# Linear attention and a softplus MLP on one core: the first unit loaded in two transfers, fewer filler matmuls at the start, and another order of the last block's last two tiles

## The chip, the cores and the metric

One Trainium2 chip, one core. The metric is device time in microseconds (us) of one launch. The kernel before took 1006.22 us, the median of 3 runs (1006.0 to 1007.1).

## The reference

The inputs are q, k and v (8 batches, 8 heads, 576 tokens, 64 columns), omega (128 features x 64), and the two weight matrices of an MLP (512 x 2048 and 2048 x 512). Cut to what matters:

```python
def phi(x):                                  # x is q or k, scaled by 64 ** -0.25
    h = x @ omega.T - sum(x * x) / 2
    return exp(h - max(h)) / sqrt(128)
kv = einsum("bhsm,bhsd->bhmd", phi(k), v)
z = phi(k).sum(axis=2)
x = einsum("bhsm,bhmd->bhsd", phi(q), kv) / (einsum("bhsm,bhm->bhs", phi(q), z) + 1e-6)
h = x.reshape(4608, 512) @ w_in              # heads side by side
out = softplus(h) @ w_out                    # 4608 x 512
```

## The kernel before, in words

The host lays the inputs out so that each transfer is one rectangle of 128 partitions. The attention of a batch is worked in two **quads** of four heads, and a quad in five **units** of 128 tokens. For a unit of keys of the first batch one transfer (line 463, 128 x 772 words) brings three things side by side: 256 columns of the transposed inputs, which PE multiplies by omega (`project`, line 491, tile `ppk`); 256 columns of the same inputs by rows, which ACT squares (line 474) and DVE sums into norms (line 481); and v with a column of ones, which the outer product with the features uses (line 700, tile `kt`). From `ppk` DVE takes the maxima (line 541), forms two biases (lines 548 and 553, tile `smk`), and ACT takes the exponents (line 561) from PSUM into the unit's own tile. Each unit needs two PSUM banks for `ppk`, and there are eight banks, so the fifth unit's `project` waits for the exponents of the first one.

The MLP takes the tokens in blocks: two of 256, then blocks of 512. Layer 1 gives `h`, ACT and DVE make the softplus, split in a high and a low part (`gh`, `gl`, or both in `g`), and layer 2 (lines 1109 to 1111: high x high, high x low, low x high) adds into four accumulators `acc`, one per **tile** of 128 tokens, over 16 **steps** of 128 hidden columns. The last two blocks are worked together (`plan_both`). The very last one has all its `g` before layer 2 starts, so its layer 2 is written out as a list, `order`: tile after tile (tt = 0 to 3), 16 steps each. Only the last tile is different: steps 0 to 12 (`LATE` = 12) at full width into its accumulator, then steps 13 to 15 for the left 256 columns, then steps 13 to 15 for the right 256 columns into a bank of its own, `right`.

`plan_out` ends a tile: DVE copies the left half of the accumulator into an output tile `o` (line 1121), ACT the right half (line 1126), and SP stores it with two transfers of 64 rows (line 1139). For tile 3 of the last block ACT copies the right half of steps 0 to 12 early, DVE copies the left half when its steps end, and DVE adds the bank `right` at the very end (line 1130); each half then goes out in two transfers, one from SP and one from ACT's queue.

Nothing of the order is left to run time. All pieces of work are planned as `Work` with a cost, a due time, the engines that can do it and the buffers that it takes and gives back. `in_order` simulates the engines with these costs and writes the one order in which instructions are emitted. An output tile of the last block takes a buffer of the room "end" at its first copy and gives it back when its last store is planned to have landed. That room has four names; three of them (`ph.0` to `ph.2`) are held to the end of the program by the sums of `plan_both`, so one, `x.0`, is left.

`with_fill` then puts **filler matmuls** (line 1582, 128 x 128 of ones with no use, two instructions each) into PE's stream where the plan has PE idle: for a gap it counts the gap less `FILL`, divided by 0.2135 us, and ahead of each work that takes a bank before `DENSE` = 12 us of planned time it puts two more. Ten fillers stand ahead of everything else.

Of the kernel before, what the change touches and what calls it, by code (L numbers as in the profile page):

```python
# [24 lines left out]
DM = 512  # L25
DFF = 2048
NFC = DFF // P
# [8 lines left out]
MARGIN = 0.0000  # L36
START = {"SP": 0.75, "ACT": 1.9, "PE": 4.6}
SLOW = 7.19
FILL = 0.3
DENSE = 12  # L40
PATIENCE = {"PE": 0.0000, "DVE": 0.00, "ACT": 0.1822, "POOL": 0.00, "SP": 3.0950}
LEAN = {"DVE": 0.2675, "POOL": 0.1608, "ACT": 0.00}
SPREAD = ((0, 10.51), (17, 12.01))
VW = 512 + 4 * (D + 1)
# [8 lines left out]
LATE = 12  # L53
# [8 lines left out]
def by(key, due):  # L62

    return due + DUE[key][PHASE[0]]
# [192 lines left out]
def with_fill(out, held, banks, until, emit):  # L257

    last, all_ = None, []
    for i, w in enumerate(out):  # L260
        if w.engine == "PE":
            t = w.end - w.cost
            n = int((t - last - FILL) / 0.2135) if last is not None and t < until else 0
            if last is not None and t < DENSE and w.take:
                n += 2
            names = [
                b for b in banks if all(x1 <= last and g < i or x0 >= t and f >= i for x0, x1, f, g in held.get(b, []))
            ] if n > 0 else []
            names = names or [box[key] for _, box, key in w.take if box[key] in banks]
            if names and n > 0:  # L270
                all_.append((emit, names[0], n))
            last = w.end
        all_.append(w)
    return all_
# [3 lines left out]
def favor_softplus_kernel(ctx, tc, q0, k0, qx, kx, tx, vv, om, wi, wo, out):  # L278
    nc = tc.nc
# [10 lines left out]
    at = ctx.enter_context(tc.tile_pool(name="at", bufs=1))  # L290
# [4 lines left out]
    def bank(name, tag):  # L295
        return ps.tile([P, 512], F32, name=name, tag=tag, bufs=1)

    idle = at.tile([P, P], F32, name="idle", tag="x.0", bufs=1)
# [38 lines left out]
    def act(n, space=None):  # L337
        return (0.066 if space == PSUM else 0.105) + 0.000833 * n

    def dve(n, rate=1):  # L340
        return 0.068 + 0.001042 * n / rate
# [4 lines left out]
    def do(engine, cost, due, emit, **kw):  # L346

        on = dict(zip(engine, cost)) if isinstance(engine, tuple) else {engine: cost}
        w = Work(on, due, emit, **kw)
        works.append(w)  # L350
        return w
# [86 lines left out]
    def plan_unit(q, kind, us, due, early, other=None):  # L438

        u = us[0]  # L440
# [3 lines left out]
        if early:  # L444
            src = (k0 if kind == "k" else q0)[q.qd]
        else:
            src = (kx if kind == "k" else qx)[q.b - 1, q.qd]
        nt = 2 * len(us) if u < 4 else 2 if other else 1
        b2 = {}
        w, n = nt * P, 2 * nt  # L450
        b = {}

        def load():
            if early:

                x = const.tile([P, 2 * DM], F32, name=f"x{nm}", tag=b["x"], bufs=1)
                b["v"] = x[:, UW : UW + 4 * (D + 1)].rearrange("p (c d) -> p c d", d=D + 1)
                b["qt"] = x[:, UW : UW + 4 * P].rearrange("p (c t) -> p c t", t=P)
                b["xs"] = x[:, : 4 * D]
                b["ph"] = x[:, : n * M].rearrange("p (c m) -> p c m", m=M)  # L460
                b["raw"], b["nat"] = x[:, :w], x[:, w : 2 * w].rearrange("p (c d) -> p c d", d=D)
                if kind == "k":
                    nc.sync.dma_start(x[:, :VW], src[:, u * VW : (u + 1) * VW])
                else:
                    nc.sync.dma_start(x[:, : 2 * w], src[:, u * UW : u * UW + 2 * w])
                return
            x = at.tile([P, 2 * UW], F32, name=f"x{nm}", tag=b["x"], bufs=1)
            nc.sync.dma_start(x[:, : 2 * w], tx[other.n - NQ] if other else src[:, u * UW : u * UW + 2 * w])
            b["raw"], b["nat"] = x[:, :w], x[:, w : 2 * w].rearrange("p (c d) -> p c d", d=D)
# [52 lines left out]
        def first(e, t):  # L522
            if not t:
                for i, x in enumerate(to):
                    x["ph"] = at.tile([P, k, M], F32, name=f"ph{nm}_{i}", tag=x["phs"], bufs=1)
            (nc.scalar.copy if e == "ACT" else nc.vector.tensor_copy)(features(t), b["pr", t][:, :, 0])
# [28 lines left out]
        def exponent(j):  # L555
# [7 lines left out]
        size = P * 4 * (VW if early and kind == "k" else 2 * w)  # L563
        ld = do(
            "SP", dma(size), by("unit.load", due), load, behind=prev.get("load"),
            take=[("w" if early else "x", b, "x")], delay=DL, spare=2 if early else 0,
        )
# [27 lines left out]
        else:  # L595
# [12 lines left out]
            for t in range(nt):  # L608
# [4 lines left out]
                c = do(  # L613
                    ("ACT", "DVE"), (act(2 * M, PSUM), dve(2 * M)), by("unit.first", due), lambda e, t=t: first(e, t), after=[p], behind=e,
                    take=[] if t else phs,
                )
# [536 lines left out]
    def plan_both(i, due, pace, box):  # L1153

        PHASE[0] = 2
        t7, t8, n = (B - 1) * MAIN, B * MAIN, TB
# [301 lines left out]
            plan_out(i, t7, tt, due + pace * NFC, acc[t7], box, [last7[tt]])  # L1458
        due += pace * NFC
        halves = [slice(k * DM // 2, (k + 1) * DM // 2) for k in range(2)]  # L1460
        order = [(tt, fc, slice(0, DM)) for tt in range(4) for fc in range(NFC if tt < 3 else LATE + 1)]
        order += [(3, fc, c) for c in halves for fc in range(LATE + 1, NFC)]
        ends = {tt: [] for tt in range(4)}
        for m, (tt, fc, c) in enumerate(order):
            w = c.stop - c.start
# [74 lines left out]
    for i, n in enumerate(sizes):  # L1540
        acc = []

        def starts(x):
            y = quads[x[1]]
            return y.b * MAIN + P * min(next(z for z in y.parts if u in z)[0] for u in x[3])

        while j < len(side) and any("q" in x[2] and starts(x) < t0 + n for x in side[j:]):
            due, m, kind, us, early = side[j]
            if kind == "kq":
                plan_unit(quads[m + 1], "k", us, due, early, quads[m])  # L1550
            else:
                plan_unit(quads[m], kind, us, due, early)
            j += 1
        boxes.append({} if i < 2 else dict(boxes[-1]))
        if t0 == (B - 1) * MAIN:
            plan_rest(at_due - 10.0)
            plan_both(i, at_due, JOINT, boxes[-1])
            break
        pace = 4.0 if i < 2 else PACE
        for fc in range(NFC):  # L1560
            plan_step(i, t0, n, fc, (FIRST + LATER * i if i < 2 else at_due) + pace * fc, pace, acc, boxes[-1])
        if i:
            at_due += (NEXT if i == 1 else pace * NFC)
        t0 += n
# [14 lines left out]
    def fill(tag, n, idle=ident):  # L1579
        t = bank("fill", tag)[:, :P]  # L1580
        for _ in range(n):
            nc.tensor.matmul(t, idle, idle, start=True, stop=True)  # L1582

    with tc.manual_schedule():
        fill("at.0", 10, idle)
        for w in with_fill(*in_order(works, room, AHEAD, MARGIN), room["any"], 70, fill):
            if isinstance(w, tuple):
                w[0](*w[1:])
                continue
            w.emit(w.engine) if len(w.on) > 1 else w.emit()  # L1590
# [99 lines left out]
```

## Time and profile before

| what | value |
|---|---|
| median of 3 runs | 1006.22 us |
| the profiled execution's own time | 1006.46 us |
| its span in the trace | 1004.7 us |
| busy PE, DVE, ACT | 992.0, 805.4, 673.7 us |
| chain that ended last: PE, DVE, ACT | 87%, 6%, 4% |

The profiled execution took 1.76 us more than its span, and 0.24 us more than the median. The chain that ended last is followed back from the last instruction, at each step to what released it, so its shares say on which engine the time was spent, and its rows say when. In the timeline a bracket gives how long the engine had been idle before the row and who ended that. Rows that follow each other on one line are merged, "x8" tells of how many. PE's matmuls overlap: their pace is read from start to start, not from their length. In these rows "PEclk" reads 1.00 throughout; a filler matmul nevertheless starts every 0.23 us in the first microseconds and every 0.13 us later, so the lower one of the clock's two levels (1.2 GHz) is read from the pace.

### The profile page before, as it was taken

What the parts mean: (1) busy time and instruction counts of PE and PEld (TensorE: products, weight loads), DVE (VectorE), ACT (ScalarE), POOL (GpSimd) and SP (SyncE); (2) the same over time, 40 slices, a digit from 0 to 9 for tenths busy, and PEclk for the clock granted to TensorE, in tenths of its full rate; (3) what the DMA queues carried; (4) which work ended last, traced back from release to release, by engine and by line L of the source; (5) the groups of instructions that cost most, each with busy time, mean ns of one, the idle gap of its engine ahead of it and who ended that gap; (6) DMA issues with size and microseconds to landing.
All of it is one profiled execution on the core that took longest, in us unless ns stands there. A gap on an engine that the chain in (4) does not pass through costs nothing.

```text
span 1004.7 us, 17142 instructions
## 1 busy us (share of the span) xinstructions
PE 992.0 (99%) x5753; PEld 807.7 (80%) x5753; DVE 805.4 (80%) x2194; ACT 673.7 (67%) x1629; POOL 79.8 (8%) x90
## 2 busy tenths in 40 slices
PE   9999999999999999999999999999999999999998
PEld 8888888787778787887878787878788778788886
DVE  6999997988868787888888897979889846998600
ACT  6999987757677675666675756756576555777600
POOL 0113211000001000100000000100010000001000
PEclk9999999999999999999999999999999999999999
DMA  9963444443252424442343335243534121000011
GB/s 346 373 242 118 146 151 122 134 117 94 96 149 95 134 93 132 137 114 82 115 120 126 91 95 152 95 132 94 133 117 112 64 79 42 1 1 1 1 53 32
DMA packets 64334, 113.81 MB, mean 113 GB/s; under 512 B 18268, under 2 KB 37112, under 8 KB 64248
## 3 DMA queue, kind: packets, MB, share of 16 engines
q1 hardware_dynamic: 64088, 112.60, 36.1%
q8 instruction: 46, 0.75, 0.3%
q14 instruction: 40, 0.33, 0.1%
q10 hardware_dynamic: 160, 0.13, 0.1%
HBM read 85.68 MB, written 27.03 MB: 112 GB/s over the span
## 4 chain that ended last, share of the span: by engine, by line
PE 87%; DVE 6%; ACT 4%; DMA 1%; issue 1%; POOL 0%; DVEq 0%; ACTq 0%; SPq 0%
PE acc L1109 13%; PE acc L1110 12%; PE acc L1111 12%; PE h L1049 10%; PE h L1050 9%; PE h L1051 9%; PE ppk L491 3%; PE kt L655 3%; PE xp L977 3%; PE pb L1384 2%; PE ppq L516 2%; PE pc L1384 2%; PE pa L1384 1%; DMA xq<-qx 1%; PE fill L1582 1%
## 5 line engine op out<-in xcount | busy, mean ns | idle before, releaser
L1109 PE MATMUL acc<-wo,gh 128*128 128x512 f32 x512 | 204.1, 399 | 0.0
L1110 PE MATMUL acc<-wo,gh 128*128 128x512 f32 x512 | 200.2, 391 | 0.0
L1111 PE MATMUL acc<-wo,gl 128*128 128x512 f32 x512 | 199.7, 390 | 0.0
L1049 PE MATMUL h<-xh,wi 128*128 128x512 f32 (+1 forms) x512 | 190.8, 373 | 1.9 <-DVE u L1064 1.1
L1050 PE MATMUL h<-xl,wi 128*128 128x512 f32 (+1 forms) x512 | 186.1, 364 | 0.0
L1051 PE MATMUL h<-xh,wi 128*128 128x512 f32 (+1 forms) x512 | 185.8, 363 | 0.0
L1055 ACT ACTIVATE u<-h 128x512 f32<-128x512 f32 (+1 forms) x128 | 70.1, 547 | 81.4 <-PE h L1051 79.2
L1109 PEld LDWEIGHTS acc<-wo,gh 128*128 128x128 f32 x512 | 96.2, 188 | 24.9 <-issue 6.8
L1049 PEld LDWEIGHTS h<-xh,wi 128*128 128x128 f32 x512 | 96.4, 188 | 23.4 <-DVE u L1064 3.9
L1111 PEld LDWEIGHTS acc<-wo,gl 128*128 128x128 f32 x512 | 96.1, 188 | 21.2 <-DVE gl L1204 0.4
L1110 PEld LDWEIGHTS acc<-wo,gh 128*128 128x128 f32 x512 | 96.5, 188 | 15.9
L1051 PEld LDWEIGHTS h<-xh,wi 128*128 128x128 f32 x512 | 96.4, 188 | 15.4
L1050 PEld LDWEIGHTS h<-xl,wi 128*128 128x128 f32 x512 | 96.6, 189 | 13.5
L1064 DVE SCALAR_TENSOR_TENSOR u<-h,u 128x512 f32<-128x512 f32 (+1 forms) x128 | 79.2, 619 | 32.7 <-ACT u L1061 31.5
L1068 ACT CAST gh<-u 128x512 fp32r<-128x512 f32 (+1 forms) x101 | 57.2, 566 | 46.0 <-PE acc L1110 29.1
L1072 DVE TENSOR_TENSOR gl<-u,gh 128x512 fp32r<-128x512 f32 (+1 forms) x106 | 68.7, 648 | 14.9 <-ACT gh L1068 13.1
L1061 ACT ACTIVATE u<-u 128x512 f32<-128x512 f32 (+1 forms) x128 | 74.2, 580 | 3.9
L1058 ACT ACTIVATE u<-u 128x512 f32<-128x512 f32 (+1 forms) x128 | 74.3, 581 | 3.2
L887 DVE CUSTOM_DVE_ANT_0 junk<-phq,zb 128x128 bf16<-128x128 f32 (+1 forms) x228 | 67.4, 296 | 7.0 <-ACT phq L561 0.4
L538 ACT ACTIVATE phq<-phq,smq 128x128 f32<-128x128 f32 x194 | 59.5, 389 | 10.1 <-DVE smq L553 10.1
L561 ACT ACTIVATE phk<-ppk,smk 128x128 f32<-128x128 f32 x230 | 63.6, 375 | 3.3 <-DVE smk L553 3.1
L541 DVE TENSOR_REDUCE smk<-ppk 128x4 f32<-128x512 f32 (+2 forms) x80 | 46.0, 595 | 24.5 <-PE ppk L491 24.5
(217 smaller groups left out, 1764.2 us busy)
## 6 DMA issues: line engine op xcount, KB each, us to landing
xk<-kx SPq DMA_DIRECT2D x28, 512.0 KB, 3.8
xq<-qx SPq DMA_DIRECT2D x28, 512.0 KB, 3.6
fdq<-flq SPq DMA_DIRECT2D x28, 512.0 KB, 2.8
qq<-fdq SPq DMA_DIRECT2D x112, 128.0 KB, 2.9
rawi<-wi SPq DMA_DIRECT2D x16, 512.0 KB, 6.7
rawo<-wo SPq DMA_DIRECT2D x16, 512.0 KB, 10.1
out<-o SPq DMA_DIRECT2D x32, 256.0 KB, 2.1
v<-vv SPq DMA_DIRECT2D x14, 576.0 KB, 3.7
```

The lines of the kernel that those rows point to most:

```text
L887: nc.vector.tensor_tensor_reduce(jk[r, c % jk.shape[1]], ph[r, c], q.zb[r, h], 1.0, 1e-6, ALU.mult, ALU.add, dn[r, 0, c : c + 1])
L1049: nc.tensor.matmul(b["h"], wh, xh[:, cc, t], start=cc == 0, stop=False)
L1050: nc.tensor.matmul(b["h"], wh, xl[:, cc, t], start=False, stop=False)
L1051: nc.tensor.matmul(b["h"], wl, xh[:, cc, t], start=False, stop=cc == NCC - 1)
L1055: nc.scalar.activation(b["u"], b["h"], AF.Abs)
L1058: nc.scalar.activation(b["u"], b["u"], AF.Exp, scale=-1.0)
L1061: nc.scalar.activation(b["u"], b["u"], AF.Ln, bias=1.0)
L1064: nc.vector.scalar_tensor_tensor(b["u"], b["h"], 0.0, b["u"], ALU.max, ALU.add)
L1072: (nc.vector if e == "DVE" else nc.gpsimd).tensor_tensor(b["gl"], b["u"], b["gh"].bitcast(F32), ALU.subtract)
L1109: nc.tensor.matmul(dst, gh, w2[fc][:, 0, c], start=start, stop=False, **kw)
L1110: nc.tensor.matmul(dst, gh, w2[fc][:, 1, c], start=False, stop=False, **kw)
L1111: nc.tensor.matmul(dst, gl, w2[fc][:, 0, c], start=False, stop=stop, **kw)
```

## The change

Three things are done. The transfer of the very first unit (quad 0, unit 0, keys) is cut in two, the 256 columns for PE first, then the other 516. Fillers: 6 instead of 10 ahead of everything, `FILL` is 1.0 instead of 0.3, and the two extra ones for works that take a bank are gone. And `order` of the last block: tile 2 stops after step 12, tile 3 goes up to step 12, then come steps 13 to 15 of tile 2, then those of tile 3's halves.

```diff
--- before.py
+++ after.py
@@ -36,8 +36,7 @@
 MARGIN = 0.0000
 START = {"SP": 0.75, "ACT": 1.9, "PE": 4.6}
 SLOW = 7.19
-FILL = 0.3
-DENSE = 12
+FILL = 1.0
 PATIENCE = {"PE": 0.0000, "DVE": 0.00, "ACT": 0.1822, "POOL": 0.00, "SP": 3.0950}
 LEAN = {"DVE": 0.2675, "POOL": 0.1608, "ACT": 0.00}
 SPREAD = ((0, 10.51), (17, 12.01))
@@ -261,8 +260,6 @@
         if w.engine == "PE":
             t = w.end - w.cost
             n = int((t - last - FILL) / 0.2135) if last is not None and t < until else 0
-            if last is not None and t < DENSE and w.take:
-                n += 2
             names = [
                 b for b in banks if all(x1 <= last and g < i or x0 >= t and f >= i for x0, x1, f, g in held.get(b, []))
             ] if n > 0 else []
@@ -460,7 +457,8 @@
                 b["ph"] = x[:, : n * M].rearrange("p (c m) -> p c m", m=M)
                 b["raw"], b["nat"] = x[:, :w], x[:, w : 2 * w].rearrange("p (c d) -> p c d", d=D)
                 if kind == "k":
-                    nc.sync.dma_start(x[:, :VW], src[:, u * VW : (u + 1) * VW])
+                    for c in ((0, w), (w, VW)) if not q.qd and not u else ((0, VW),):
+                        nc.sync.dma_start(x[:, c[0] : c[1]], src[:, u * VW + c[0] : u * VW + c[1]])
                 else:
                     nc.sync.dma_start(x[:, : 2 * w], src[:, u * UW : u * UW + 2 * w])
                 return
@@ -1458,7 +1456,8 @@
             plan_out(i, t7, tt, due + pace * NFC, acc[t7], box, [last7[tt]])
         due += pace * NFC
         halves = [slice(k * DM // 2, (k + 1) * DM // 2) for k in range(2)]
-        order = [(tt, fc, slice(0, DM)) for tt in range(4) for fc in range(NFC if tt < 3 else LATE + 1)]
+        order = [(tt, fc) for tt in range(2) for fc in range(NFC)] + [(tt, fc) for tt in (2, 3) for fc in range(LATE + 1)]
+        order = [(tt, fc, slice(0, DM)) for tt, fc in order + [(2, fc) for fc in range(LATE + 1, NFC)]]
         order += [(3, fc, c) for c in halves for fc in range(LATE + 1, NFC)]
         ends = {tt: [] for tt in range(4)}
         for m, (tt, fc, c) in enumerate(order):
@@ -1582,7 +1581,7 @@
             nc.tensor.matmul(t, idle, idle, start=True, stop=True)
 
     with tc.manual_schedule():
-        fill("at.0", 10, idle)
+        fill("at.0", 6, idle)
         for w in with_fill(*in_order(works, room, AHEAD, MARGIN), room["any"], 70, fill):
             if isinstance(w, tuple):
                 w[0](*w[1:])
```

The fillers on PE fall from 10, 1, 1, 1, 6, 5, 2, 18, 1 to 6, 0, 0, 0, 1, 0, 0, 15, 0; the one of 18 stands some 61 us into the program. Nothing else of any engine's order changes between the start and the last block. The rows below are from PE around the fifth and sixth unit (`ppk_0_2`: quad 0, unit 2), first before, then with the change.

```order
L491 MATMUL ppk_1_1_1_160<-omf,xk_1_1_112 128x128
L1582 MATMUL fill<-ident 128x128 x6
L491 MATMUL ppk_0_2_0_189<-omf,xk_0_2_123 128x128
L491 MATMUL ppk_0_2_1_190<-omf,xk_0_2_123 128x128
L491 MATMUL ppk_0_2_0_189<-omf,xk_0_2_123 128x128
L491 MATMUL ppk_0_2_1_190<-omf,xk_0_2_123 128x128
L1582 MATMUL fill<-ident 128x128 x5
L491 MATMUL ppk_1_2_0_216<-omf,xk_1_2_137 128x128
L491 MATMUL ppk_1_2_1_217<-omf,xk_1_2_137 128x128
L491 MATMUL ppk_1_2_0_216<-omf,xk_1_2_137 128x128
L491 MATMUL ppk_1_2_1_217<-omf,xk_1_2_137 128x128
```

```order
L489 MATMUL ppk_1_1_1_151<-omf,xk_1_1_109 128x128
L1581 MATMUL fill<-ident 128x128
L489 MATMUL ppk_0_2_0_175<-omf,xk_0_2_120 128x128
L489 MATMUL ppk_0_2_1_176<-omf,xk_0_2_120 128x128
L489 MATMUL ppk_0_2_0_175<-omf,xk_0_2_120 128x128
L489 MATMUL ppk_0_2_1_176<-omf,xk_0_2_120 128x128
L489 MATMUL ppk_1_2_0_196<-omf,xk_1_2_132 128x128
L489 MATMUL ppk_1_2_1_197<-omf,xk_1_2_132 128x128
L489 MATMUL ppk_1_2_0_196<-omf,xk_1_2_132 128x128
L489 MATMUL ppk_1_2_1_197<-omf,xk_1_2_132 128x128
```

The block of six fillers is one, the block of five is gone, so nothing stands between the two projections.

The next rows are from PE in the last block, where tile 3 has ended step 12; `acc_3` and `acc_2` are the accumulators of tiles 3 and 2, `g_12` the step's softplus, and in brackets the engine that an instruction waits for. First before, then with the change.

```order
L1109 MATMUL acc_3_10680<-wo_1586,g_12_10377 128x512
L1110 MATMUL acc_3_10680<-wo_1586,g_12_10377 128x512
L1111 MATMUL acc_3_10680<-wo_1586,g_12_10377 128x512
L1109 MATMUL acc_3_10680<-wo_1782,g_13_10343 128x256
L1110 MATMUL acc_3_10680<-wo_1782,g_13_10343 128x256
L1111 MATMUL acc_3_10680<-wo_1782,g_13_10343 128x256
L1109 MATMUL acc_3_10680<-wo_1817,g_14_10477 128x256 [waits Activation_49]
L1110 MATMUL acc_3_10680<-wo_1817,g_14_10477 128x256
```

```order
L1109 MATMUL acc_3_10643<-wo_1558,g_12_10349 128x512
L1107 MATMUL acc_2_10598<-wo_1754,g_13_10315 128x512
L1108 MATMUL acc_2_10598<-wo_1754,g_13_10315 128x512
L1109 MATMUL acc_2_10598<-wo_1754,g_13_10315 128x512
L1107 MATMUL acc_2_10598<-wo_1789,g_14_10449 128x512
L1108 MATMUL acc_2_10598<-wo_1789,g_14_10449 128x512
L1109 MATMUL acc_2_10598<-wo_1789,g_14_10449 128x512
L1107 MATMUL acc_2_10598<-wo_1853,g_15_10428 128x512
L1108 MATMUL acc_2_10598<-wo_1853,g_15_10428 128x512
L1109 MATMUL acc_2_10598<-wo_1853,g_15_10428 128x512
L1107 MATMUL acc_3_10643<-wo_1754,g_13_10315 128x256 [waits Activation_49]
```

Before, the second half-width step waits for ACT; now nine full-width matmuls of tile 2 lie between step 12 and the first half-width step, and that one carries the wait.

The last rows are from DVE, the copies out of the last block's tiles, up to DVE's last instruction; DMAHW are transfers that have to have landed. First before, then with the change.

```order
L1121 COPY o_0_10576<-acc_0_10515 128x256 [waits PE_49,Pool_49]
L1121 COPY o_1_10630<-acc_1_10572 128x256 [waits DMAHW0_49,DMAHW1_49,PE_49,Activation_49]
L1121 COPY o_2_10684<-acc_2_10626 128x256 [waits DMAHW2_49,DMAHW3_49,PE_49,Activation_49]
L1121 COPY o_3_10728<-acc_3_10680 128x256 [waits DMAHW4_49,DVE_49,DMAHW5_49,PE_49,Activation_49]
L1130 TENSOR_TENSOR o_3_10728<-right,o_3_10728 128x256 [waits PE_49]
```

```order
L1119 COPY o_0_10548<-acc_0_10487 128x256 [waits PE_49,Pool_49]
L1119 COPY o_1_10602<-acc_1_10544 128x256 [waits DMAHW1_49,DMAHW2_49,PE_49,Activation_49]
L1119 COPY o_3_10686<-acc_3_10643 128x256 [waits DMAHW3_49,DVE_49,DMAHW4_49,PE_49,Activation_49]
L1128 TENSOR_TENSOR o_3_10686<-right,o_3_10686 128x256 [waits PE_49]
L1119 COPY o_2_10719<-acc_2_10598 128x256 [waits DMAHW6_49,DMAHW5_49,DMAHW7_49,DMAHW0_49,DVE_49]
```

Tile 2's copy stood ahead of tile 3's; now it is the last instruction, and it waits for four transfers, which are the four stores of tile 3. ACT's copy of tile 2 and SP's two stores of it have moved behind tile 3's in the same way.

## Rows read from the trace of the kernel before

**Rows 1.** Chain of waits, 0 to 140 us (start us, length us, what).

```profile
27.14 0.66 PE kt L695 x4
...
27.82 0.39 ACT kvs L706
...
56.39 0.42 DVE u L1064
...
102.77 0.39 PE h L1049
```

**Rows 2.** Timeline of PE and SP's queue, start (start us, us, engine, line, operation).

```profile
1.05 4.64 PE L1582 MATMUL fill<-idle 128*128 128x128 f32 x20 [1.05 <-DVE marks L321]
...
1.19 5.65 SPq L463 DMA_DIRECT2D xk<-k  x10
...
5.75 1.20 PE L491 MATMUL ppk<-omf,xk 64*128 64x128 f32 x8
...
10.45 1.60 PE L1582 MATMUL fill<-ident 128*128 128x128 f32 x12
...
14.27 0.79 PE L491 MATMUL ppk<-omf,xk 64*128 64x128 f32 x8
...
16.79 0.72 PE L491 MATMUL ppk<-omf,xk 64*128 64x128 f32 x8
```

**Rows 3.** Timeline of ACT, start (in brackets: idle before, and who ended it).

```profile
4.54 0.42 ACT L474 ACTIVATE xk<-xk 128x256 f32<-128x256 f32 x1 [2.53 <-DMA xk<-k]
...
9.75 1.23 ACT L561 ACTIVATE xk<-ppk,smk 128x128 f32<-128x128 f32 x4
...
11.54 0.62 ACT L561 ACTIVATE xk<-ppk,smk 128x128 f32<-128x128 f32 x2 [0.26 <-DVE smk L553]
...
14.18 0.62 ACT L561 ACTIVATE xk<-ppk,smk 128x128 f32<-128x128 f32 x2 [0.37 <-DVE smk L553]
...
18.84 1.66 ACT L561 ACTIVATE xk<-ppk,smk 128x128 f32<-128x128 f32 x6 [1.48 <-DVE smk L553]
```

**Rows 4.** Timeline of DVE, start.

```profile
15.02 0.43 DVE L541 TENSOR_REDUCE smk<-ppk 128x2 f32<-128x256 f32 x1 [0.59 <-PE ppk L491]
...
17.54 0.76 DVE L541 TENSOR_REDUCE smk<-ppk 128x2 f32<-128x256 f32 x2 [0.71 <-PE ppk L491]
...
18.59 0.16 DVE L553 SCALAR_TENSOR_TENSOR smk<-smk 128x4 f32<-128x4 f32 x1
```

**Rows 5.** Windows: busy us of PE, PEld, DVE, ACT, POOL; PEclk, DMA share, GB/s.

```profile
20.00:22.00 2.00, 2.00 (x18) 1.65 (x17) 1.94 (x8) 2.00 (x7) 0.00 (x0) 1.00 1.07 383
```

**Rows 6.** Timeline of PE and DVE, end of the last block.

```profile
997.62 0.28 PE L1109 MATMUL acc<-wo,g 128*128 128x256 f32 x1
...
997.85 0.28 PE L1111 MATMUL acc<-wo,g 128*128 128x256 f32 x1
...
998.63 0.38 PE L1109 MATMUL acc<-wo,g 128*128 128x256 f32 x1 [0.51 <-ACT o L1126]
...
1000.41 0.28 PE L1111 MATMUL right<-wo,g 128*128 128x256 f32 x1
...
1000.73 0.42 DVE L1130 TENSOR_TENSOR o<-right,o 128x256 f32<-128x256 f32 x1 [0.59 <-PE right L1111]
```

**Rows 7.** Timeline of ACT and DVE, tiles copied out near the end.

```profile
954.73 0.37 ACT L1126 COPY o<-acc 128x256 f32<-128x256 f32 x1 [1.78 <-DVE o L1121]
...
957.30 0.42 DVE L1121 COPY o<-acc 128x256 f32<-128x256 f32 x1 [1.91 <-DMA out<-o]
...
957.76 0.37 ACT L1126 COPY o<-acc 128x256 f32<-128x256 f32 x1 [1.96 <-DVE o L1121]
...
989.49 0.37 ACT L1126 COPY o<-acc 128x256 f32<-128x256 f32 x1 [10.51 <-DVE o L1121]
```

**Rows 8.** Windows, the DMA column after the last two tiles' stores.

```profile
992.25:992.50 0.25, 0.25 (x3) 0.21 (x2) 0.00 (x0) 0.00 (x0) 0.00 (x0) 1.00 0.10 25
...
1002.50:1003.00 0.50, 0.00 (x0) 0.00 (x0) 0.00 (x0) 0.00 (x0) 0.00 (x0) 1.00 0.72 176
```

## The prediction, made before the changed kernel was run

> **What bounds the kernel now.** I read the chain of waits first, then the timeline and the windows of its two ends, because the change touches nothing between them. The chain lies on PE up to 27.8 us, then on ACT, from 56.4 us mostly on DVE, and from 102.8 us on PE to the end [rows 1]. So three engines hand the lead on, and a microsecond saved at the start is worth a microsecond only if ACT and DVE, which take over, also come earlier by it. By 20 us both are full: in the two microseconds from 20 to 22 DVE is busy for 1.94 and ACT for 2.00, and the DMA engines for 1.07 of their time, which is all of it [rows 5]. So what the start can give has to come before 20 us, as idle time of ACT and DVE that goes. At the end the reader should see that PE stalls once, at 998.63 for ACT's copy, and that after the last matmul only an addition and tile 3's stores are left [rows 6].
>
> **The start, part by part.** The fillers ahead of everything are 20 instructions in 4.64 us, 0.232 us each [rows 2]. Eight fewer is 1.86 us, so PE is through at 3.8 instead of 5.7. The first projection could start when the first 128 KB have landed; the whole unit, issued at 1.19, had landed at 4.54, when ACT squared it [rows 2, 3]. This 1.2 to 1.9 us earlier projection I count at nothing by itself. ACT's first squares still wait for the second part of the unit and for the units behind it, and these come no sooner while DMA is the bound. The extra issue costs between nothing and one issue, 5.65 / 10 = 0.57 us [rows 2]. I take nothing, since SP is ahead of the data here; if DMA were not full, ACT's squares would be later by that 0.57.
>
> The Trainium skill, "DMA: Bandwidth & Descriptors", "Rules for kernel authors", says to merge many small transfers into one large one, which speaks against the cut. By that rule the 0.57 us would count, and the sum below would be 0.57 us worse; no row here shows a cut load.
>
> The fillers that matter are those ahead of the fifth and later units. 12 instructions run from 10.45 for 1.60 us, ten more follow, and the sixth unit's projection starts only at 14.27 [rows 2]. Without them something else holds it: the banks. The fifth unit needs the banks of the first unit's exponents, the first half of the four from 9.75, so 9.75 + 0.61 = 10.4. The sixth takes a bank that the exponents of 11.54 give back at 12.16 [rows 3], so it runs at about 12.3 and its maxima on DVE come at about 13.3 instead of 15.02 [rows 4]. The seventh unit's projection stood at 16.79 [rows 2]. It needs a bank of the exponents that ran at 14.18 after 0.37 idle [rows 3]; without that idle time they end at 13.81 + 0.62 = 14.4, the projection starts at 14.5, 2.3 us earlier, and one outer product ahead of it fits in between. Its maxima move from 17.54 to about 15.2, and the bias that ended at 18.59 + 0.16 = 18.75 [rows 4] is there at 16.5.
>
> ACT waited 1.48 us for that bias, until 18.84. So its own queue was free at 17.36 [rows 3], and less the 0.37 it is free at 17.0, after the bias. Both waits go: 0.37 + 1.48 = **1.85 us**. That is what I take as gained at 20 us and, with ACT and DVE full from there [rows 5], handed on to PE at 102.8 [rows 1] and to the end. At most the 0.26 ahead of 11.54 [rows 3] goes too, which makes 2.11; at least it is nothing, if something later than 20 us, a load above all, holds the work where it was. I take 1.85 because both ACT waits are named and the replacement times clear them. The three fewer fillers of the block of 18, at some 61 us, count at nothing, as DVE has the lead there [rows 1].
>
> **The end, part by part.** First the gain. The 18 half-width matmuls start between 997.62 and 1000.41, 2.79 us [rows 6]. The first three start at 997.62 to 997.85, 0.115 apart, so 17 steps take 2.0. The stall is therefore 0.8 us, of which 0.51 is marked as idle for ACT's copy. I take 0.78. With the change nine full-width matmuls of tile 2, twice as wide and so about 2 us, lie between step 12 and the first half, and ACT's copy, 0.37 long, ends under them. The stall goes: **-0.78 us**. These nine are moved, not added.
>
> Then the loss. Output tiles of the last block share one buffer. In the new order tile 3 takes it first, at its step 12, and holds it until its stores have landed. Tile 2, whose matmuls end 2 us ahead of the last one, may be copied out only then, and the order shows it: its DVE copy is the last one, and waits for four transfers. So after the final addition the program now does, one after another, what it used to do in tile 2's own time.
>
> - Tile 3's stores land. After 954.73 + 0.37 = 955.10 a stored buffer could be written again at 957.30, 2.20 us later [rows 7]. These were larger stores; the last bytes of tile 3's went out before 1003.0, at most 1.85 us after the addition's end at 1001.15 [rows 6, 8]. I take 2.2, as a wait ends after the bytes.
> - DVE copies the left half, 957.30 to the start of ACT's at 957.76, 0.46; ACT copies the right half, 0.37 [rows 7]. Together 0.83.
> - SP stores tile 2 in two transfers. After the same copy before, which ended at 989.49 + 0.37 = 989.86 [rows 7], the last bytes went between 992.25 and 992.50 [rows 8], say 2.45 us.
>
> That is 2.2 + 0.83 + 2.45 = 5.48 us from the addition's end to the last byte, where 1.85 stood: **+3.63 us**. With a 1.85 us landing it is 3.28; if the four waits cost one store issue of half a microsecond more, 4.1. With the stall, the end is worth +2.85, between +2.4 and +3.4.
>
> **The sum.** -1.85 + 2.85 = +1.0. The profiled execution's 1006.46 becomes 1007.46; it stands 0.24 above the median of 1006.22, so against the median the forecast is **1007.2 us**.
>
> **The rivals.**
>
> *PE's clock stays at the lower level (slower).* The fillers kept PE busy while the units came in. Its pace was 0.232 us per filler up to 5.7 us and 0.133 from 10.45 on, and the first projection took 1.20 us where later ones took 0.72 [rows 2]; PEclk reads 1.00 over the whole stretch, so the level is read from the pace. With the fillers gone PE works about 0.7 in each 1.2 us between 6 and 10 us. If the clock has not risen by the sixth unit at 12.3, its projection, the outer product and the seventh projection take 0.5, 1 and 0.5 us more, and the bias of 16.5 comes at 18. Of the 1.85 us about 0.8 are left. The time would be 1006.22 + 2.85 - 0.8 = 1008.3, just over the bound, and nearer 1008.7 if the outer products behind stay slow too. For it: this is the place where fillers were put densest. Against it: PE is busy from 1.05 without a gap until after 5 us either way. It decides from the point where the seventh projection starts after 15.5. Chance 0.13. [...]
>
> *The start gives nothing (slower).* A full DMA [rows 5] means that loads come when they come. If weights or query units after 20 us become what ACT and DVE wait for, the gain is taken back there, and 1006.22 + 2.85 = 1009.1. Against it: neither engine has an idle stretch that ended with a load between 9 and 55 us. Chance 0.12.
>
> *The end costs nothing (faster).* If the last copy did not wait for tile 3's stores, tile 2's copies and stores would lie under the half-width matmuls as before, and 1006.22 - 1.85 - 0.78 = 1003.6. For it: tile 2's matmuls end 2 us before the last. Against it: the four transfers that the copy waits for. Chance 0.05.
>
> **How the numbers follow.** The forecast, with the two terms between their bounds (0.1 to 1.9 us slower), has 0.70. A measurement of this kernel can tell 0.2%, 2.0 us, from no change. So all of the forecast is "same", the two slower rivals lie beyond +2.0 and have 0.25, and faster by more than that has 0.05. The range goes from 1006.0, where the start gives 2.1 and the end costs 2.4, less 0.5 for what I may have missed among the first units, to 1009.1, where the start gives nothing.
>
> **What would show it.** The sixth projection near 12.3 and the seventh near 14.5, ACT's idle 1.48 before the eighteenth microsecond gone, and the chain changing from DVE to PE near 101 instead of 102.8. At the end: no stall between step 12 and the halves, then DVE idle for about 2.2 us after the addition until a store lands, one copy each on DVE and ACT, and two stores, the last instruction of DVE being tile 2's copy. It is wrong if tile 2's copy runs before the addition, if the projections are no earlier, or if PE reaches its lead at 102.8 as before.

## The result, and the profile after

| | before | changed |
|---|---|---|
| median | 1006.35 us (4 runs, 1006.0 to 1007.1) | 1020.57 us (4 runs, 1019.98 to 1021.2) |
| profiled execution | 1006.46 us | 1021.09 us |
| its span | 1004.7 us | 1019.3 us |
| its mean granted TensorE clock | 0.999 | 0.978 |

The ratio is 1.0137, with a 95% interval of 1.0121 to 1.0153: **14 us slower**, where 1.0 was forecast, and far outside the range. Runs of a kernel with thinned fillers differ among themselves by several microseconds, so the medians below stand with their ranges.

The timeline of PE at the start of the changed kernel (start us, length us, engine, line, operation, in brackets the idle time before and who ended it):

```profile
1.05 2.93 PE L1581 MATMUL fill<-idle 128*128 128x128 f32 x12 [1.05 <-DVE marks L318]
4.04 1.23 PE L489 MATMUL ppk<-omf,xk 64*128 64x128 f32 x8
6.12 0.71 PE L489 MATMUL ppk<-omf,xk 64*128 64x128 f32 x8 [0.86 <-DMA xk<-k]
8.72 2.18 PE L489 MATMUL ppk<-omf,xk 64*128 64x128 f32 x16 [1.89 <-DMA xk<-k]
10.86 0.77 PE L1581 MATMUL fill<-ident 128*128 128x128 f32 x2
11.69 2.62 PE L489 MATMUL ppk<-omf,xk 64*128 64x128 f32 x16
14.24 1.97 PE L698 MATMUL kt<-xk 128*128 128x65 f32 x8
16.14 1.23 PE L489 MATMUL ppk<-omf,xk 64*128 64x128 f32 x8
```

The first projection takes 1.23 us and the second 0.71, so the clock rose between them. PE then stands idle for 1.89 us, and from the third unit on everything is at the slow pace again: 1.23 us for a projection, 1.97 for the eight outer products of a unit that took 1.11 in kernels whose clock is up (e8_dense, below). The windows say for how long (columns as in [rows 5]):

```profile
8.00:8.50 0.50, 0.00 (x0) 0.00 (x0) 0.00 (x0) 0.00 (x0) 0.00 (x0) 1.00 0.93 352
8.50:9.00 0.50, 0.28 (x2) 0.28 (x4) 0.00 (x0) 0.30 (x1) 0.00 (x0) 0.77 1.02 408
9.00:12.00 3.00, 2.94 (x20) 2.39 (x21) 2.85 (x13) 2.40 (x10) 0.00 (x0) 0.50 1.03 409
...
40.00:49.50 9.50, 9.50 (x50) 8.39 (x50) 6.70 (x24) 4.96 (x13) 0.00 (x0) 0.50 0.50 179
49.50:49.75 0.25, 0.25 (x4) 0.25 (x2) 0.15 (x1) 0.25 (x2) 0.00 (x0) 0.53 0.32 131
49.75:52.00 2.25, 2.25 (x22) 2.00 (x22) 1.30 (x4) 2.23 (x8) 0.69 (x1) 1.00 0.67 198
```

The granted clock falls to 0.50, 1.2 GHz, within 8.5 to 9.0 us, just as PE takes up work again, and is back at 2.4 GHz only from 49.75 us. In between PE has no idle row: it is busy for 9.50 of the 9.50 us of the long window, at 5.3 matmuls per microsecond, and at 9.8 in the window after the rise. DVE and ACT, which were full at 20 us before [rows 5], are busy for 6.70 and 4.96 of the 9.50. The chain of waits shows the consequence (start us, length us, what):

```profile
49.31 0.73 PE kt L693 x4
50.09 0.26 issue
50.35 0.37 ACT xh L843
...
69.31 0.42 DVE u L1062
...
115.23 0.42 DVE u L1062
115.69 0.39 PE h L1047
```

PE holds the lead until 50.0 us instead of 27.8; ACT hands over to DVE at 69.31 instead of 56.39, and PE takes the lead for good at 115.69 instead of 102.77 [rows 1]. That is 12.9 us late, and nothing behind it makes it good but for 1.6 us.

The end, in the timeline of DVE and ACT:

```profile
1010.25 0.42 DVE L1119 COPY o<-acc 128x256 f32<-128x256 f32 x1 [20.37 <-PE acc L1109]
1011.28 0.42 DVE L1128 TENSOR_TENSOR o<-right,o 128x256 f32<-128x256 f32 x1 [0.60 <-PE right L1109]
1014.04 0.42 DVE L1119 COPY o<-acc 128x256 f32<-128x256 f32 x1 [2.34 <-DMA out<-o]
1014.54 0.37 ACT L1124 COPY o<-acc 128x256 f32<-128x256 f32 x1 [7.04 <-DVE o L1119]
```

This is the forecast sequence: the addition, 2.34 us of waiting for a store of tile 3, a copy each on DVE and ACT, two stores, and nothing after.

To split the difference I use two marks in all kernels: in the timeline of PE, the first behind 100 us and the last of the groups of 32 outer products (tile `kt`, "128x128 f32 x32"). Everything of the start lies ahead of the first mark, the whole end behind the last.

| profiled execution | first mark | last mark | span | last mark to end |
|---|---|---|---|---|
| before | 115.37 | 760.34 | 1004.7 | 244.36 |
| changed | 128.28 | 771.66 | 1019.3 | 247.64 |
| e1_end | 116.07 | 760.87 | 1008.5 | 247.63 |
| e2_start | 131.72 | 775.34 | 1019.7 | 244.36 |
| e3_cut | 115.13 | 759.68 | 1004.0 | 244.32 |
| e4_fill | 125.69 | 769.52 | 1013.8 | 244.28 |
| e5_gap | 112.69 | 756.54 | 1000.9 | 244.36 |
| e6_buf | 114.76 | 759.96 | 1003.8 | 243.84 |
| e7_head | 118.69 | 761.86 | 1006.1 | 244.24 |
| e8_dense | 113.76 | 758.20 | 1002.5 | 244.30 |
| e9_hold | 113.72 | 756.78 | 1004.4 | 247.62 |
| e10_head10 | 122.65 | 765.46 | 1013.1 | 247.64 |
| e11_best | 113.00 | 756.54 | 1000.4 | 243.86 |
| e13_late10 | 113.02 | 755.88 | 1003.5 | 247.62 |
| e14_late6 | 115.39 | 758.21 | 1005.8 | 247.59 |

The changed kernel is 12.91 us late at the first mark and 11.32 at the last, and loses 247.64 - 244.36 = 3.28 behind it. 11.32 + 3.28 = 14.60, the difference of the two spans.

### The profile page after: what moved, and what is told of

It is laid out like the page before. It is cut to its first block, busy times and chain, and to the rows that moved or that the text cites. A ratio compares the mean times of both kernels' runs of the same rounds, so it can differ in the third digit from the quotient of the medians.

```text
span 1019.3 us, 17048 instructions
## 1 busy us (share of the span) xinstructions
PE 1001.1 (98%) x5707; PEld 817.1 (80%) x5707; DVE 805.7 (79%) x2194; ACT 675.1 (66%) x1629; POOL 80.0 (8%) x90
## 4 chain that ended last, share of the span: by engine, by line
PE 88%; DVE 5%; ACT 3%; DMA 2%; issue 1%; SPq 0%; DVEq 0%; ACTq 0%
PE acc L1107 12%; PE acc L1108 12%; PE acc L1109 12%; PE h L1047 10%; PE h L1048 9%; PE h L1049 9%; PE ppk L489 3%; PE kt L653 3%; PE xp L975 3%; PE pb L1382 2%; PE ppq L514 2%; PE pc L1382 1%; PE kt L698 1%; PE pa L1382 1%; PE ppq L489 1%
```

## The experiments

"Fillers" are counted as in the code; each is two matmuls. The comparisons are with runs of the kernel before on the same chip, whose median lay between 1006.35 and 1006.66 us.

### First, the parts one by one

The question was whether the end costs what I had said, and whether the loss at the start comes from the removed fillers or from the cut load, since in the profile the third unit was squared at 8.70, later than before.

**e1_end**: the kernel before with the new order of the last block alone.

```diff
-        order = [(tt, fc, slice(0, DM)) for tt in range(4) for fc in range(NFC if tt < 3 else LATE + 1)]
+        order = [(tt, fc) for tt in range(2) for fc in range(NFC)] + [(tt, fc) for tt in (2, 3) for fc in range(LATE + 1)]
+        order = [(tt, fc, slice(0, DM)) for tt, fc in order + [(2, fc) for fc in range(LATE + 1, NFC)]]
```

> The kernel before with the new order of the last block alone. Theory A (tile 2 waits for tile 3's stores, the price is the one of the changed kernel's trace): from the first half-width matmul to the end of the span 10.37 us there against 7.08 before, so +3.3, 1009.6 us. The forecast's own term was +2.85, 1009.2. Rival: the end is hidden after all and only the stall goes, -0.8, 1005.6.

Measured: 1010.72 us (5 runs, 1009.73 to 1011.56), ratio 1.0041, 1.0028 to 1.0053. The end costs, and by the profile exactly what it costs in the changed kernel: 247.63 us behind the last mark. That is 3.27 of the median's 4.4, and within the interval (2.8 to 5.3 us); in the profile another 0.53 lies ahead of the last mark.

**e2_start**: all of the change but the order of the last block.

> The changed kernel with the old order of the last block: the cut load and the fewer fillers alone. Theory A (the loss is PE's lower clock from 8.7 to 49.7 us): 1020.6 less the 3.3 of the end, 1017.3 us, with PEclk 0.50 from about 9 to 50 us as in the changed kernel. Rival: start and end do not add up, and what one costs the other hides; then it is off 1017.3 by more than 1 us.

Measured: 1016.45 us (4 runs, 1012.28 to 1021.55), ratio 1.0101, 1.0068 to 1.0134. So the start alone loses 6 to 15 us, and the median is within 1 us of theory A's 1017.3. The clock did not do what theory A says, though. In the profile, which is that of the slowest run (1021.55), it did not fall at 9 us; the slow pace is there from the start:

```profile
6.14 3.75 PE L490 MATMUL ppk<-omf,xk 64*128 64x128 f32 x24 [0.55 <-DMA xk<-k]
...
10.67 2.50 PE L490 MATMUL ppk<-omf,xk 64*128 64x128 f32 x16
13.10 1.97 PE L699 MATMUL kt<-xk 128*128 128x65 f32 x8
```

24 matmuls of three projections take 3.75 us, 1.25 for each projection, and the outer products 1.97. By the pace the clock rose only between 60 and 62 us.

**e3_cut**: the kernel before with the first load in two transfers, alone.

```diff
-                    nc.sync.dma_start(x[:, :VW], src[:, u * VW : (u + 1) * VW])
+                    for c in ((0, w), (w, VW)) if not q.qd and not u else ((0, VW),):
+                        nc.sync.dma_start(x[:, c[0] : c[1]], src[:, u * VW + c[0] : u * VW + c[1]])
```

> The kernel before with the load of the first unit in two transfers and nothing else; all fillers stay. Theory A: the cut costs at most one issue, 0 to 0.6 us, 1006.4 to 1007.0, and the clock stays up. Theory B (the cut makes the third unit land at 8.7 instead of 7.15 us): the third unit's square on ACT starts 1 us or more later than 7.15, and the time is 1007 to 1008.

Measured: 1006.46 us (11 runs, 1004.85 to 1009.02), ratio 1.0004, 0.9994 to 1.0013. The cut neither gives nor costs anything that can be measured, and theory B falls: the third unit's square starts at 7.22 us.

**e4_fill**: the three edits of the fillers alone (6 instead of 10 at the start, `FILL` = 1.0, no pairs), with the old load and the old end.

> The kernel before with the fewer fillers and nothing else; the first load is whole. Theory A (fillers alone decide): the clock falls near 9 us as in the changed kernel, 1017 us or so. Theory B (the cut opens the gap of 1.9 us ahead of the third unit, and that gap lets the clock fall): PE waits for the third unit 0.3 us only, the clock stays at its upper level, and the 1.85 us of my forecast come in, 1004.5 us.

Measured: 1013.8 us (4 runs, 1011.08 to 1016.08), ratio 1.0065, 1.004 to 1.0089. The removed fillers alone do it, so the cut is not needed for the loss. They do it later than theory A had it: in the profile the projection at 9.74 runs at the fast pace, and the granted clock falls between 12.5 and 13.0 us.

```profile
9.74 1.23 PE L489 MATMUL ppk<-omf,xk 64*128 64x128 f32 x10
```

```profile
12.50:13.00 0.50, 0.50 (x5) 0.50 (x5) 0.50 (x3) 0.50 (x4) 0.00 (x0) 0.61 1.02 403
```

### Which fillers

**e5_gap**: `FILL` = 1.0 alone.

> The kernel before with gaps of up to 1.0 us, instead of 0.3 us, left without fillers; the 10 at the start and the two more per gap in the first 12 us stay. Theory H (the first stretch decides): the clock rises as before, the time is 1006.4 or up to 1.9 us less. Theory D (the fillers ahead of the fifth to seventh units keep the clock): the short runs of 2 to 3 fillers leave gaps, the clock falls at 9 to 13 us and the time is 1010 to 1020, by less if part of the gaps are still filled.

Measured: 1002.96 us (5 runs, four from 1002.48 to 1003.36 and one of 1026.46 with a mean granted clock of 0.972), ratio without that one 0.9962, 0.9949 to 0.9975. So shorter filler runs do give time here in four runs of five. The fifth has no trace; its mean granted clock points at the low level.

**e7_head**: 6 instead of 10 at the start, alone.

```diff
-        fill("at.0", 10, idle)
+        fill("at.0", 6, idle)
```

> The kernel before with 6 instead of 10 fillers asked for at the very start, everything else as it was. Theory H (the length of the first stretch of PE work decides whether the clock rises): PE's first projections run with gaps, the clock stays or falls to the lower level for many us, and the time is 1012 to 1020. Theory D (the fillers ahead of the fifth to seventh units keep the clock): these are there, so the clock is up from about 10 us on and the time is 1006.4, within 0.2%.

Measured: 1007.65 us (10 runs, 1003.74 to 1008.87), ratio 1.0006, 0.9994 to 1.0017. The time is theory D's, within 0.2%, but the clock is not up from 10 us on; theory H falls by its time:

```profile
4.70 1.23 PE L491 MATMUL ppk<-omf,xk 64*128 64x128 f32 x8 [0.72 <-DMA xk<-k]
...
14.87 1.29 PE L491 MATMUL ppk<-omf,xk 64*128 64x128 f32 x8
16.09 1.43 PE L1582 MATMUL fill<-ident 128*128 128x128 f32 x10
17.57 0.78 PE L491 MATMUL ppk<-omf,xk 64*128 64x128 f32 x8
```

After twelve matmuls and 0.72 us of waiting the projections are at 1.23 us, and stay there until 15 us; the ten matmuls from 16.09 run at the fast pace, and so does all behind. The late rise costs 3.3 us at the first mark, of which 1.5 are left at the last. So in this profile the clock rises later with the shorter start, and it rises under the later fillers of this kernel. Two of the ten runs took 1003.74 and 1003.96, the others 1007.36 and more.

**e8_dense**: no pairs ahead of works that take a bank, alone.

```diff
-            if last is not None and t < DENSE and w.take:
-                n += 2
```

> The kernel before without the rule that adds two fillers to each gap of the first 12 us; the 10 at the very start stay. Theory H (the first stretch decides): the clock rises as before, the time is 1006.4 or, with the fillers out of the way of the projections, up to 1.9 us less (1004.5). Theory D (the fillers ahead of the fifth to seventh units keep the clock): the clock falls at about 9 to 13 us and the time is 1010 to 1020.

Measured: 1004.08 us (6 runs, 1002.96 to 1005.27), ratio 0.9972, 0.9961 to 0.9983. The timeline of PE:

```profile
8.18 0.72 PE L489 MATMUL ppk<-omf,xk 64*128 64x128 f32 x8 [1.76 <-DMA xk<-k]
...
10.32 1.13 PE L1580 MATMUL fill<-ident 128*128 128x128 f32 x8 [0.42 <-issue]
11.51 0.78 PE L489 MATMUL ppk<-omf,xk 64*128 64x128 f32 x8
12.22 0.94 PE L1580 MATMUL fill<-ident 128*128 128x128 f32 x6
13.22 0.79 PE L489 MATMUL ppk<-omf,xk 64*128 64x128 f32 x8
13.93 1.11 PE L698 MATMUL kt<-xk 128*128 128x65 f32 x8
```

A wait of 1.76 us, nearly that of the changed kernel, does not let this clock fall. What stands behind it are 14 matmuls ahead of the fifth and the sixth unit, where the changed kernel has 2.

**e10_head10**: the changed kernel with the 10 at the start restored.

> The changed kernel with one part undone: 10 instead of 6 fillers asked for at the very start. Theory H (those four, eight matmuls, decide; with them PE is busy from 1.05 us until the clock has risen, and the gaps behind do no harm): the clock is up from about 5.5 us on, ACT's two waits of the start are gone, and the time is the 1006.4 of the kernel before, less the 2.4 to 3.5 that the start gave with 10 fillers, plus the 4.3 of the changed end: 1007.2 to 1008.3. Theory S (gaps add up: without both the added pairs and the short runs the clock falls whatever stood at the start): 1013 to 1021, as with the changed kernel.

Measured: 1015.95 us (6 runs, 1014.32 to 1021.48), ratio 1.0105, 1.0084 to 1.0125. Theory H falls, and the time is where theory S had it: the four fillers at the start do not save the changed kernel.

```profile
5.74 1.18 PE L490 MATMUL ppk<-omf,xk 64*128 64x128 f32 x16
8.00 0.72 PE L490 MATMUL ppk<-omf,xk 64*128 64x128 f32 x8 [1.08 <-DMA xk<-k]
8.98 0.71 PE L490 MATMUL ppk<-omf,xk 64*128 64x128 f32 x8 [0.26 <-DMA xk<-k]
10.14 0.46 PE L1582 MATMUL fill<-ident 128*128 128x128 f32 x2 [0.44 <-issue]
10.66 1.26 PE L490 MATMUL ppk<-omf,xk 64*128 64x128 f32 x10
12.37 1.01 PE L490 MATMUL ppk<-omf,xk 64*128 64x128 f32 x6 [0.45 <-ACT xk L560]
13.31 1.97 PE L699 MATMUL kt<-xk 128*128 128x65 f32 x8
```

Up to 12 us the clock is up. Then, after four waits of 0.26 to 1.08 us, the outer products are at 1.97. The windows show the fall and how long the low level lasts, with PE busy all the time:

```profile
12.50:13.00 0.50, 0.50 (x6) 0.50 (x6) 0.47 (x4) 0.50 (x3) 0.00 (x0) 0.63 1.05 420
13.00:35.00 22.00, 22.00 (x111) 19.38 (x111) 13.66 (x50) 12.68 (x44) 0.80 (x2) 0.50 1.04 402
```

That waits alone add up to a fall is not shown by this, as the fillers that would stand between them are gone too.

**e9_hold**: the changed kernel with 8 fillers ahead of the third unit, where PE had stood idle for 1.89 us.

```diff
+            count += 1
...
+            n = {3: 8}.get(count, n)
```

> The changed kernel with 8 fillers (16 matmuls) put ahead of the third unit's projection, where PE stood idle for 1.89 us in the profile of the changed kernel; 6 fillers at the start, as in it. Theory I (the idle time ahead of the third unit lets a clock fall that had risen): the clock is up by about 8 us and stays, and the time is 1006.4 - 2 + 4.3 = 1007 to 1009. Theory H (the first stretch of 12 fillers with the wait behind it is too little, and what follows finds the clock low): the rise comes later, as it came after some 15 us with the shorter first stretch alone, the time is 1010 or more and differs from run to run.

Measured: 1016.53 us (7 runs: one of 1006.23, which is the profiled one, the others from 1015.77 to 1018.85), ratio 1.0086, 1.0061 to 1.0111. In the one run the clock held (mean granted clock 0.997). The six have no trace, but their mean granted clocks of 0.985 to 0.988 say that it did not, so the idle time ahead of the third unit is not the cause alone.

**e13_late10** and **e14_late6**: the changed kernel with 4 and 3 fillers, 14 matmuls, ahead of the fifth and the sixth unit, as e8_dense has them; with 10 at the start, and with the 6 of the changed kernel.

```diff
+            count += 1
...
+            n = {5: 4, 6: 3}.get(count, n)
```

> The changed kernel with 10 fillers at the start and, ahead of the fifth and the sixth unit's projection, 4 and 3 fillers (14 matmuls), where the changed kernel has one and none. Theory L (the gaps between the fourth and the sixth unit, from about 9.5 to 12.5 us, are what lets a clock fall that had risen): the clock stays up, and the time is 1006.6 - 2.4 + 4.3 = 1008.5, or up to 1.5 less. Theory C (the cut of the first unit's load or the moved end, which the kernel with pairs alone removed did not have, takes part): 1013 to 1021 still, with the clock falling at about 12.8 us.

> The changed kernel with 4 and 3 fillers (14 matmuls) ahead of the fifth and the sixth unit's projection and still 6 at the start. If the gaps at 9.5 to 12.5 us decide alone: 1008 to 1010. If the start decides as well, since PE then waits ahead of the second and third units with the clock barely up or not up: the clock is low at 10 us, the rise comes later, and the time lies between 1010 and 1021, above that of the kernel with 10 at the start.

Measured: 1006.84 us (12 runs, 1005.29 to 1010.3; ratio 1.0008, 0.9998 to 1.0018) and 1007.49 us (10 runs, 1007.17 to 1008.62; ratio 1.0011, 1.0002 to 1.0019). Theory C falls, with the cut and the new end in both kernels. Theory L's time holds for e13_late10, to within 0.2 us of its lower bound; its profile is that of the fastest run (1005.29), and three of the twelve runs took 1009.1 to 1010.3 at mean granted clocks of 0.994 to 0.996. For e14_late6 neither case came as said: the clock is low at 10 us, as in the second, and the time is still below the first. The timeline of PE in e14_late6:

```profile
4.04 1.23 PE L492 MATMUL ppk<-omf,xk 64*128 64x128 f32 x8
6.21 1.23 PE L492 MATMUL ppk<-omf,xk 64*128 64x128 f32 x8 [0.94 <-DMA xk<-k]
8.51 2.18 PE L492 MATMUL ppk<-omf,xk 64*128 64x128 f32 x16 [1.08 <-DMA xk<-k]
10.64 2.05 PE L1584 MATMUL fill<-ident 128*128 128x128 f32 x8
12.75 0.90 PE L492 MATMUL ppk<-omf,xk 64*128 64x128 f32 x8
13.58 0.94 PE L1584 MATMUL fill<-ident 128*128 128x128 f32 x6
14.57 0.79 PE L492 MATMUL ppk<-omf,xk 64*128 64x128 f32 x8
15.29 1.11 PE L701 MATMUL kt<-xk 128*128 128x65 f32 x8
```

At 10.6 us this PE is where the changed kernel's was, at the slow pace; here the clock had not risen yet, there it had fallen at 8.5 to 9.0, ahead of the place that theory L names. The eight matmuls run slowly (0.26 us each), the projection behind them is between the levels (0.90), the six that follow are fast (0.16 each), and the outer products take 1.11. Six fillers more, 12 matmuls, are worth 13 us. So these fillers do more than hold a clock that is up: in this run they are what it rises under.

### The end, and a version that beats both

**e6_buf**: e1_end with a second buffer for the output tiles of the last block.

```diff
-    room["end"] = room["ph"] + room["x"]
+    room["end"] = room["ph"] + room["x"] + room["v"]
```

> The kernel before with the changed end alone, and a second buffer for the last block's output tiles, so that the copies of tile 2 need not wait for tile 3's stores. Theory A (the end costs what it costs because tile 2's copy waits for the landing of tile 3's stores): the wait of about 2.3 us ahead of DVE's copy is gone, tile 2 is copied and stored under the half-width matmuls, and with the stall of 0.8 us gone too the time is 1006.35 - 0.8 = 1005.6; anything from 1005.0 to 1006.4 is taken as that. Theory B (the order of the last matmuls costs by itself, through PE or through the DMA queue of the stores): the time stays near 1010.7, where the changed end alone stood, or at the least above 1008.5.

Measured: 1006.27 us (11 runs, 1004.19 to 1006.75), ratio 0.9992, 0.9983 to 1.0001. Theory A: the wait for tile 3's store was the cost.

```profile
997.50 0.42 DVE L1121 COPY o<-acc 128x256 f32<-128x256 f32 x1 [19.28 <-PE acc L1111]
998.58 0.42 DVE L1121 COPY o<-acc 128x256 f32<-128x256 f32 x1 [0.65 <-PE acc L1111]
999.60 0.42 DVE L1130 TENSOR_TENSOR o<-right,o 128x256 f32<-128x256 f32 x1 [0.59 <-PE right L1111]
```

Tile 2 is copied at 997.50, under the half-width matmuls, and the addition is the last of DVE again. Behind the last mark stand 243.84 us, 0.52 less than before: of the 0.78 of the stall 0.52 is had.

**e11_best**: `FILL` = 1.0 and the end of e6_buf; the 10 at the start and the pairs stay.

> The kernel before with gaps of up to 1.0 us left without fillers (10 at the start and the added pairs stay), and the changed end with a second buffer for the output tiles. If the two parts add up: 1006.5 - 3.5 - 0.2 = 1002.8, and 1002.2 where the removed stall of 0.8 us gives its full worth. If the start's gain hangs on luck with the clock: single runs above 1010 among others near 1002.8. If the end costs: 1003.5 or more.

Measured: 1002.25 us (5 runs, 1001.02 to 1002.42), ratio 0.9951, 0.994 to 0.9963. The two parts add up, and the kernel beats the one before and the changed one. That the clock holds every time is not shown: e5_gap has the same `FILL`, and one of its five runs took 1026.46.

## Why the prediction was wrong

**The step that failed is the price of the clock rival**, and with it the start's term of the sum: -1.85 us were forecast, and the changed kernel is 12.91 us late at the first mark and 11.32 at the last. I had named the mechanism and its place, with a chance of 0.13, and let it take only some 1.05 us: "of the 1.85 us about 0.8 are left". I priced the slow level for the sixth projection, one outer product and the seventh, as if the clock came back by itself once PE was full. It does not here: PE was busy without a row of idle time from 8.72 to 49.5 us, and at 1.2 GHz from 9.0 on. So the price is that of 40 us at half the pace in a stretch where PE then sets the pace. The sign that I gave for this rival came true: the seventh projection starts at 16.14, after 15.5.

My argument against it, that PE is busy without a gap until after 5 us, was true and beside the point. By the pace the clock did rise in the changed kernel, between 5.27 and 6.12 us, and it fell after PE had waited 0.86 and then 1.89 us, where I had counted on 0.7 us of work in each 1.2. The third unit was squared at 8.70 instead of 7.15; e8_dense, without the cut, has 8.16, so the cut is not needed for that. What lets the clock fall was not isolated (e9_hold). Nor is a fall needed for the loss: e2_start's profiled run was slow from the start and took 1021.55 us, and one of the changed kernel's four runs took 1019.98 at a mean granted clock of 0.998, where the other three have 0.978. That run has no trace.

What decides here is whether the clock is up once the units are in. e14_late6 shows this term alone: with 14 matmuls ahead of two units instead of 2, and everything else as changed, the median goes from 1020.57 to 1007.49 (ratios to the kernel before: 1.0137 and 1.0011). Why the clock rises under those and not under 40 us of projections and outer products stays open.

The Trainium skill, "TensorE: Matmul & The Clock Gate", "Why this matters for your kernels", asks to keep TensorE busy without a break first, and then to leave no long idle gaps between bursts of matmuls. Here shorter gaps came before a fall, 1.89 us at the longest in the changed kernel and 1.08 in e10_head10, and the measurement decides. In "What's actually happening" the same page of the Trainium skill has activity release the throttle and says that the point differs from run to run. On the latter the runs agree: the changed kernel and e14_late6 have the same order on PE up to the fourth unit, and the second projection takes 0.71 us in one and 1.23 in the other. On the former they agree for fillers (e7_head, e14_late6), while the projections and outer products of the changed kernel, which fill PE's row for 40 us, did not do it.

**The start's gain of 1.85 us.** Where the clock stays up, it is there. In e13_late10, with 10 at the start, no wait of ACT for a bias is left between 9 and 24 us, where before there were three, 0.26, 0.37 and 1.48 [rows 3], and the first mark comes at 113.02 instead of 115.37: 2.35, a little more than my upper bound of 2.11, which counts all three. This is the fastest of its twelve runs. In e14_late6, with 6 at the start, the sixth projection stands at 14.57 where I had said 12.3, and the first mark at 115.39, as before: the slow first 12 us take the whole gain.

**The end.** Forecast +2.85, between 2.4 and 3.4; the changed kernel's profile shows +3.28, and e1_end +3.27. The stall is gone: the last 18 matmuls start between 1008.93 and 1010.96, 2.03 us as forecast. The landing took 2.34 for 2.2, from the addition's end at 1011.70 to 1014.04. The copies took 0.87 for 0.83, up to 1014.91. From there to the end of the span are 4.39 us, where 3.55 stood behind the addition before (1004.7 - 1001.15), so the stores cost 0.84 where I had 2.45 - 1.85 = 0.60. Together 4.05 for 3.63, and 4.05 - 0.78 = 3.27.

**The middle.** I had said that the change touches nothing there. Between the two marks e14_late6 takes 642.82 us and the kernel before 644.97; the kernels with the old fillers (e1_end, e3_cut, e6_buf) lie between 644.55 and 645.20, all with other fillers between 642.81 and 644.44. So up to 2.2 us were gained in a stretch that I left out. I read that from one profile of each kernel; which wait it is was not tried. It is also why the 1007.49 of e14_late6, +0.9 on its own kernel before, meets the forecast of +1.0 by other terms: +3.2 at the end, nothing at the start, -2.15 in between.

**The other rivals.** The end does cost, so that rival was sized rightly. The cut, which I counted at nothing, is between -0.6 and +1.3 us by e3_cut's interval; that leaves the 0.57 us of one more issue open. "The start gives nothing" was the right sign for the changed kernel, for another reason than a full DMA.

## What to carry to other kernels

Idle matmuls that hold the clock are to be priced by what happens if they fail, 40 us at half pace here, and not by the work next to them; here a clock that was lost came back only after 23 us (e10_head10) to 40 us (the changed kernel) of full work. Thin them one group at a time, with several runs each: three thinnings that gave 2.4, 3.5 and about nothing apart lost 7 us together. An output tile that is finished out of order needs a buffer of its own, or it waits for a whole store.

## What the runs showed of the hardware that was not expected

- PE can be busy for 40 us and stay at 1.2 GHz (granted clock 0.50 from 9.0 to 49.5 us in the changed kernel, from 13.0 to 36 us in e10_head10). In e14_late6 the pace doubled within the 14 filler matmuls and the projection between them; under the projections and outer products of the changed kernel it took until 49.75.
- The same kernel settles on either side: in e9_hold one run took 1006.23 us at a mean granted clock of 0.997, and six took over 1015 at 0.985 to 0.988.
- The column PEclk reads 1.00 over the first 60 us of e2_start, while its projections take 1.25 us and its outer products 1.97. It shows the low level only after a fall; ahead of the first rise the level has to be read from the pace.
